# Three pairs of visits to small tensor-engine tiles joined in an attention and expert kernel

## The chip, the cores and the metric

The kernel runs on one core of one Trainium2 chip. The metric is the device time of one execution in microseconds (us); of several runs the median counts. The profiled execution is one further run of the same program.

## The reference, cut to what matters

`x` is (8, 8, 512, 64) and `state` is (8, 8, 32, 64): batch, head, position, width. Both sides read each other by attention, the two results are laid end to end along the positions, and a feed-forward layer with the mish-like gate follows.

```python
scores = scale * np.matmul(x, state.transpose(0, 1, 3, 2))
xread = softmax(scores) @ state              # (8, 8, 512, 64)
scores2 = scale * np.matmul(state, x.transpose(0, 1, 3, 2))
sread = softmax(scores2) @ x                 # (8, 8, 32, 64), "the state read"
attn = np.concatenate([xread, sread], axis=2)
x = attn.transpose(0, 2, 1, 3).reshape(8 * 544, 512)
h = x @ w_in                                 # (4352, 2048)
g = h * np.tanh(softplus(h))
out = g @ w_out                              # (4352, 512)
```

## The kernel before, in words

The work goes batch by batch (0 to 7), and each batch goes through eight **slots** of 256 columns of the hidden layer. `w_in` is folded with the state beforehand: `sw_slice` (from line 575) multiplies a slot of `w_in` with the batch's state blocks `bds[b]`, so that the first product of a slot (`gemm1`, the tile `ph`) multiplies the batch's softmax weights `ah`, `al` with that small matrix. Values are kept as a rounded part and a rest (`gh`/`gl`, `ah`/`al`, `swh`/`swl`), so most products come three times. The second product (`gemm2` in batch 0, `consume` later; tiles `acc...`) adds g times `w_out` into four PSUM banks.

Beside these full 128x128 matmuls stand **visits** to small tiles of the tensor engine, all plain f32, each of which the profile counts in two passes per matmul:

- `sw_slice`, the visit of one or two slots: weights of 64 rows and 32 columns, 16 passes for one slot and 32 for two. Its first step issues the matmuls into two banks of the pool `misc` (two banks in all), its second step copies them out on ScalarE (`act.copy` to `swh`), its third subtracts on VectorE (`dve.tensor_sub` to `swl`, or `sw` where both parts share a tile). The banks are free again after the third step.
- `scores` (from line 335), the scores of batches 1 to 7: the same 64x32 tiles, 32 passes into two banks, then a scaling of one bank on ScalarE and of the other on VectorE. It needs `xTs`, whose rows (`x_rows`) eight DMAs of `x_moved` (line 306) bring from `x_turned`, which VectorE wrote by transposing.
- `sread(kc)`, the state read: weights of 128 rows and 32 columns, 32 passes for each of two `kc`, into a bank of the pool of `ph` (two banks, `first_bank`). It needs `e2T`, which `e2_turned` (line 403) brings with 16 DMAs from `u`, which VectorE wrote by transposing the exponentials. Its second step scales on VectorE into `srds`.

**What sets the order.** Every compute engine but SyncE is wrapped in `InOrder` (line 59): each instruction is chained behind the one the program issued before on that engine. The order is written out by hand as lists of step names. Batch 0 is one long list (`hi3`, `sw6`, `SC`, ...; lower case steps are those of batch 0, `SC`, `TR`, `EX` and so on those of batch 1). Batches 1 to 7 have eight lines each in `TABLE`, one line per slot; a line that a batch lacks is taken from "steady". Naming a step once more runs its generator on to the next `yield`, so the first `S2` issues the matmuls, the second the ScalarE copies, the third the VectorE subtractions. Only the order of the DMA queue of SyncE (SP) is left to the planner of the framework; it took them here in the order of the program as they became ready.

Step names used below: `z0 z1` the state read of batch 0 (within batch 1's table), `sr0 sr1` that of the batch at hand, `SR0 SR1` that of the next batch, which the table of batch 6 uses once for batch 7, the last of its state reads. `S2` the visit of slots 2 and 3, `N0` that of slot 0 of the next batch. `mm`, `ee`, `tu`: maximum, exponential and turning (`e2_turned`) for the state read. `X0` to `X3` the four transposes to `x_turned`, `XD` the eight DMAs to `x_rows`. `A` and `B`: half of a slot's second products (in slots 0 and 1 of batch 1 they end batch 0, and each copies two results `o` out, the even one on VectorE and the odd one on ScalarE). `G0 G1` first products, `M0 M1` the activations behind them. `P p` preparing of a unit for the second product. `PR` the weights `ah`, `al`. `w0` to `w5` writes and loads of `w_in` by SP.

Of the kernel before, what the change touches and what calls it, by code (L numbers as in the profile page):

```python
# [17 lines left out]
P = 128  # L18
B, H, S, NS, D = 8, 8, 512, 32, 64
# [36 lines left out]
def half(par):  # L56
    return slice(par * D, (par + 1) * D)
# [23 lines left out]
def state_attention_mish_kernel(ctx, tc, x, state, w_in, w_out, out):  # L81
# [193 lines left out]
    def attention(b, sn, x_in=None):  # L275
# [60 lines left out]

        def scores():

            pss = [(misc if b < 3 else first_bank)(f"sc_{b}_{u}") for u in range(2)]
            for kc in range(2):  # L340
                kp = slice(kc * 2 * P, (kc + 1) * 2 * P)
                for c in range(NC):
                    o = slice(c * NS, (c + 1) * NS)
                    for u in range(2):
                        last["PE"] = pe.matmul(
                            pss[u][o, kp].rearrange("n (t v g) -> n t v g", t=NT, v=2), bds[b][half(u), kc, o],
                            xTs[c][half(u), :, kc].rearrange("p v (t g) -> p t v g", t=NT), start=True, stop=True)
            yield

            scs = pool.tile([P, 2, S], F32, tag="sc", name=f"scs_{b}", bufs=1)  # L350
            for kc in range(2):
                sc[kc] = scs[:, kc]

            for u in range(2):
                o = scs.rearrange("n k (t v u p) -> n (k t) v u p", t=NT, v=2, u=2)[:, :, :, u]
                i = pss[u].rearrange("n (k v p) -> n k v p", v=2, p=32)
                if u:
                    dve.tensor_scalar_mul(o, i, 0.125)
                else:
                    act.mul(o, i, 0.125)  # L360
                if b == 1:
                    yield
# [134 lines left out]
        def sread(kc):  # L497
# [17 lines left out]

        own = dict(
            x=x_transposed, st=lambda _: state_blocks(b, sn() if b == 1 else sn) if b else state_blocks_0(sn), sc=lambda _: scores() if b else scores_q(), tr=soft1_t, ex=soft1_x,
            no=lambda _: soft1_n(), pr=soft1_a, mm=soft2_m, ee=soft2_e, sr=sread, xd=lambda _: x_moved(), tu=lambda _: e2_turned(), fill=fill, aT=aT)

# [354 lines left out]
    for step in """  # L874
            st st st x0 x1 ldi0 x2 x3 sc hia0 ldi1 acc sc sc sc hib0 sc dia0 tr0 tr0 tr1 tr0 ldo0 tr1 jia0 cib0
            tr1 st ex0 ex1 jib0 no fill6 sw0 cib1 cia1 no coa0 ldi2 sw0 fill2 ldo1 pr0 pr0 hia1 ldi4 pr1 ldi3
            dob0 pr0 hib1 pr1 sw0 hoa0 qa0 qb0 ldo2 ldi5 jia1 jib1 di2 hob0 hi2 fill2 pr1 sw1 sw1 qb1 qa1 ji2
            ldo3 fill2 sw1 ma0 joa0 mb0 job0 ko1 ma0 mb0 wha0 sw2 p1 lx co1 loa0 sw2 la0 ci3 m1 ldo4 whb0 ga0
            lb0 sw2 lob0 ko1 ldo5 ga0 ga0 ja1 ga0 gb0 hi3 ho2 m1 ji3 gb0 gb0 lg1 ja1 gb0 p2 ci4 co2 ldo6 ldi6
            lo1 do3 sw3 g1 jo2 sw3 hi4 ji4 jo2 sw3 lo2 n2 g1 n2 X1 ho3 lg2 ldi7 g1 X2 jo3 p3 mm1 hi5 ho4 m3 sw4  # L880
            di5 g1 X3 sw4 jo3 g2 ji5 co4 sw4 g2 m3 ho5 lo3 jo4 lg3 ST X0 g2 jo4 g2 co5 sw5 p4 sw5 n4 sw5 hi6 di6
            lo4 n4 XD0 ja5 ci7 g3 g3 ja5 g3 lg4 p5 ji6 m5 g3 g4 mm0 ee0 SC SC lo5 hi7 ee1 xi2 g4 sw6 m5 g4 SC
            lg5 ldo7 sw6 TR1 g4 ji7 sw7 ho6 ee0 sw6 p6 ho7 co6 ee1 TR0 g5 TR1 g5 TR0 EX1 tu EX0 ja6 sw7 n6 co7 g5
            n6 NO xz0 sw7 ja6 g5 NO PR0 xy0 next lg6 lo6 p7 PR0 PR1 g6 g6 n7 PR0 PR1 next g6 ja7 PR1 n7
            g6 next ja7 lg7 lo7
            """.split():
        what, i = re.fullmatch(r"([a-zA-Z]+)(\d*)", step).groups()
        if not hasattr(begun.get(step), "send"):
            begun[step] = steps[what](int(i or 0))
        if hasattr(begun[step], "send"):  # L890
            next(begun[step], None)

    A12, A22, A11, A21 = range(4)
    S1, S3, S2, S4 = range(3, 7)
# [178 lines left out]
    def half_slot(key, j, at):  # L1073
# [4 lines left out]
        elif ready and (ready[0][:2] != (key, 0) or ready[0][2] < j + (j == SLOTS - 1 and at)):  # L1078
# [1 line left out]

    TABLE = {
        1: """
            G0 M0 G1 M1 z0 z1 mm0 mm1 ee0 ee1 A z0 z1 ee0 ee1 tu X0 X1
            P G0 M0 p G1 M1 w0 S2 S2 S2 X2 X3 XD B ST w1
            P G0 M0 p G1 M1
            P G0 M0 p G1 M1 S4 S6 A S4 S4 S6 S6 T0 T0
            P G0 M0 p G1 M1 sr0 sr1 SC SC A sr0 sr1 SC MM0 MM1 w2 lx TR0 TR1 TR0 TR1
# [34 lines left out]
            P G0 M0 p G1 M1 P p TR0 TR1 A P TR0 TR1 p B  # L1122
            P G0 M0 p G1 M1 S6 sr0 sr1 P p S6 S6 sr0 sr1 ly w2 EE0 EE1 EX0 EX1 A EE0 EE1 TU P p B NO
            P G0 M0 p G1 M1 P p NO PR0 PR1 A P p B
            P G0 M0 p G1 M1 N0 PR0 PR1 P p N0 N0 A P p SR0 SR1 SR0 SR1 w3 rs B U rt W0 A W1 P p""",
        B - 1: """
            P G0 M0 p G1 M1 P p A P p w4 B
            P G0 M0 p G1 M1 S2 P p S2 S2 w5 A P p B
# [133 lines left out]
```

## Time and profile before

| | before |
|---|---|
| median of 3 runs | 626.93 us (626.0 to 627.03) |
| profiled execution, its own time | 625.96 us |
| span from first to last instruction | 624.2 us |
| PE busy | 617.3 us (99%) |
| PEld (weight loads) busy | 533.9 us (86%) |
| DVE / ACT / POOL busy | 447.5 / 368.3 / 232.2 us |
| mean granted clock of TensorE | 1.000 |

PE is TensorE's matmuls, PEld its weight loads, which lie beside them; DVE is VectorE, ACT ScalarE, POOL GpSimd, SP SyncE, which here only issues DMAs. A busy share is an average; matmuls are pipelined and overlap, so the distance from one start to the next tells what one costs. In a timeline a row is: start in us, length in us, engine, line, operation, output<-inputs, shape, count; in brackets the idle time of the engine before it and what ended it ("issue": nothing that the profile shows). Nearly all rows carry line 73, that of the helper which records each operation, so tiles tell them apart.

### The profile page before, as it was taken

The numbers are of one execution on the slowest core, as the hardware profiler recorded it, in microseconds if no ns is written. First come the engines' busy times: TensorE is split into PE (matmuls) and PEld (weight loads), VectorE is DVE, ScalarE is ACT, GpSimd is POOL, SyncE is SP. The second block draws the span as 40 slices with busy tenths as digits, with TensorE's granted clock in tenths as the row PEclk, the third lists the DMA queues.
The fourth block names the chain that finished last, engine by engine and source line by source line (L and its number), as shares of the span: only waits on it lengthen the run. The fifth ranks groups of instructions, "written<-read, shape, count | busy, mean of one in ns | idle before, by whom it ended". The sixth has DMA issues, their size and how long they took to land.

```text
span 624.2 us, 13824 instructions
## 1 busy us (share of the span) xinstructions
PE 617.3 (99%) x5388; PEld 533.9 (86%) x5388; DVE 447.5 (72%) x764; ACT 368.3 (59%) x764; POOL 232.2 (37%) x348
## 2 busy tenths in 40 slices
PE   8999999999999999999999999999999999999997
PEld 6777677788888898898988898889889899898897
DVE  5999976766678885968667774869387787535364
ACT  5999876466457355565547555655456766544442
POOL 0000000235366065326632573246522744443284
PEclk9999999999999999999999999999999999999999
DMA  9995922944452163534554265415455332320011
GB/s 330 412 339 165 357 71 78 305 146 123 117 195 70 33 172 115 160 114 128 146 169 135 68 155 168 165 54 154 119 172 164 108 109 96 102 68 25 11 35 35
DMA packets 71969, 88.79 MB, mean 142 GB/s; under 512 B 13792, under 2 KB 49120, under 8 KB 71904
## 3 DMA queue, kind: packets, MB, share of 16 engines
q1 hardware_dynamic: 71472, 87.71, 44.8%
q8 instruction: 43, 0.70, 0.5%
q10 hardware_dynamic: 432, 0.20, 0.1%
q14 instruction: 22, 0.18, 0.1%
HBM read 62.85 MB, written 13.11 MB: 122 GB/s over the span
## 4 chain that ended last, share of the span: by engine, by line
PE 87%; ACT 2%; DVE 1%; DMA 1%; issue 1%; SPq 0%; DVEq 0%
PE ph L73 25%; PE acc_top L73 15%; PE acc_one L73 11%; PE acc_two L73 11%; PE acc_end L73 9%; PE swp L73 5%; PE ph_s L73 4%; PE acc L73 3%; PE srp L73 1%; PE acc_s_one L73 1%; PE acc_s_top L73 1%; PE acc_s_two L73 1%; PE sc L73 1%; DMA out_dram<-o 1%; PE acc_s_end L73 0%
## 5 line engine op out<-in xcount | busy, mean ns | idle before, releaser
L73 POOL TENSOR_TENSOR sums<-u 128x256 f32<-128x256 f32 x96 | 78.1, 814 | 194.0 <-DVE gl L73 118.8
L73 DVE TENSOR_TENSOR gl<-u,gh 128x384 fp32r<-128x384 f32 (+1 forms) x112 | 70.7, 631 | 69.5 <-ACT gh L73 62.7
L73 ACT ACTIVATE u<-ph 128x256 f32<-128x256 f32 x224 | 73.6, 382 | 79.3 <-PE ph L73 77.8
L73 POOL TENSOR_TENSOR sums<-sums,u 128x128 f32<-128x128 f32 x192 | 112.7, 587 | 15.1
L73 DVE TENSOR_TENSOR gl<-sums,gh 128x512 fp32r<-128x512 f32 x96 | 78.1, 813 | 30.6 <-ACT gh L73 30.6
L73 ACT CAST gh<-u 128x384 fp32r<-128x384 f32 (+1 forms) x112 | 59.2, 529 | 67.0 <-PE acc_end L73 49.3
L73 PE MATMUL acc_top<-wo,gh 128*128 128x256 f32 (+1 forms) x448 | 93.5, 300 | 0.0
L73 POOL TENSOR_TENSOR w_sums<-w_sums 128x256 f32<-128x256 f32 x28 | 25.2, 902 | 151.7 <-DMA x_rows<-x_turned 110.8
L73 ACT CAST gh<-sums 128x512 fp32r<-128x512 f32 x96 | 59.6, 621 | 32.2 <-POOL sums L73 32.1
L73 PEld LDWEIGHTS acc_top<-wo,gh 128*128 128x128 f32 x448 | 71.2, 191 | 4.5 <-issue 1.6
L73 PE MATMUL ph<-ah,swh 128*128 128x512 f32 (+1 forms) x228 | 70.5, 391 | 0.0
L73 PE MATMUL ph<-al,swh 128*128 128x512 f32 (+1 forms) x228 | 69.9, 388 | 0.2 <-DVE al L73 0.2
L73 PE MATMUL ph<-ah,swl 128*128 128x512 f32 (+1 forms) x228 | 69.9, 388 | 0.0
L73 PE MATMUL acc_top<-wo,gl 128*128 128x256 f32 (+1 forms) x224 | 66.9, 298 | 0.0
L73 PEld LDWEIGHTS ph<-al,swh 128*128 128x128 f32 x228 | 42.5, 188 | 10.0 <-DVE al L73 0.4
L73 PEld LDWEIGHTS ph<-ah,swl 128*128 128x128 f32 x228 | 42.6, 188 | 9.3
L73 DVE TENSOR_TENSOR swl<-swp,swh 128x512 fp32r<-128x512 f32 (+1 forms) x60 | 36.3, 645 | 18.5 <-ACT swh L73 18.5
L73 PEld LDWEIGHTS ph<-ah,swh 128*128 128x128 f32 x228 | 39.5, 188 | 8.3 <-issue 0.8
L73 PEld LDWEIGHTS acc_top<-wo,gl 128*128 128x128 f32 x224 | 42.7, 191 | 1.4
L73 ACT CAST swh<-swp 128x512 fp32r<-128x512 f32 (+1 forms) x60 | 30.5, 564 | 17.2 <-PE swp L73 17.2
L73 PE MATMUL acc<-wo,gh 128*128 128x512 f32 x128 | 40.3, 396 | 0.0
L73 PE MATMUL acc_one<-wo,gh 128*128 128x256 f32 x192 | 39.8, 289 | 0.0
(233 smaller groups left out, 1394.1 us busy)
## 6 DMA issues: line engine op xcount, KB each, us to landing
w_in<-w_in_again SPq DMA_DIRECT2D x27, 1024.0 KB, 6.1
x<-in_x_dram SPq DMA_DIRECT2D x32, 256.0 KB, 4.4
wir<-in_moe_w_in_dram SPq DMA_DIRECT2D x16, 512.0 KB, 9.4
wor<-in_moe_w_out_dram SPq DMA_DIRECT2D x16, 512.0 KB, 8.6
x_rows<-x_turned SPq DMA_DIRECT2D x56, 128.0 KB, 2.4
out_dram<-sums SPq DMA_DIRECT2D x25, 256.0 KB, 4.6
x_in<-in_x_dram SPq DMA_DIRECT2D x24, 256.0 KB, 4.8
w_in_again<-w_in_sb SPq DMA_DIRECT2D x4, 1024.0 KB, 7.5
```

What stands on the lines that cost most here:

```text
L73: made = method(*args, **kwargs)
```

## The change

Only the order of steps changes, and in one place the banks that a step takes:

- Batch 0's list: the first step of `sw6` (its matmuls) goes ahead of the two `SC` of batch 1, so that the slot visit and the scores of batch 1 follow each other on TensorE without other matmuls between. As the slot visit then holds the two `misc` banks, the scores of batch 1 take the two `first_bank` banks instead. The second and third steps of `sw6` stay where they were.
- Batch 1's table: the three steps of `S2` move from the second line into the first: the matmuls right behind `z0 z1`, the ScalarE copies behind `A`, the VectorE subtractions behind the second steps of `z0 z1` and ahead of the second steps of `ee0 ee1` and of `tu`.
- Batch 6's table, last line: `SR0 SR1` move from behind the first half of the slot's second products (`A P p`) to the place ahead of `N0`; their second steps go ahead of those of `N0`, and the load `w3` goes ahead of `A`.

```diff
-            pss = [(misc if b < 3 else first_bank)(f"sc_{b}_{u}") for u in range(2)]
+            pss = [(misc if b == 2 else first_bank)(f"sc_{b}_{u}") for u in range(2)]
...
-            lo4 n4 XD0 ja5 ci7 g3 g3 ja5 g3 lg4 p5 ji6 m5 g3 g4 mm0 ee0 SC SC lo5 hi7 ee1 xi2 g4 sw6 m5 g4 SC
+            lo4 n4 XD0 ja5 ci7 g3 g3 ja5 g3 lg4 p5 ji6 m5 g3 g4 mm0 ee0 sw6 SC SC lo5 hi7 ee1 xi2 g4 m5 g4 SC
             lg5 ldo7 sw6 TR1 g4 ji7 sw7 ho6 ee0 sw6 p6 ho7 co6 ee1 TR0 g5 TR1 g5 TR0 EX1 tu EX0 ja6 sw7 n6 co7 g5
...
         1: """
-            G0 M0 G1 M1 z0 z1 mm0 mm1 ee0 ee1 A z0 z1 ee0 ee1 tu X0 X1
-            P G0 M0 p G1 M1 w0 S2 S2 S2 X2 X3 XD B ST w1
+            G0 M0 G1 M1 z0 z1 S2 mm0 mm1 ee0 ee1 A S2 z0 z1 S2 ee0 ee1 tu X0 X1
+            P G0 M0 p G1 M1 w0 X2 X3 XD B ST w1
             P G0 M0 p G1 M1
             P G0 M0 p G1 M1 S4 S6 A S4 S4 S6 S6 T0 T0
             P G0 M0 p G1 M1 sr0 sr1 SC SC A sr0 sr1 SC MM0 MM1 w2 lx TR0 TR1 TR0 TR1
...
-            P G0 M0 p G1 M1 N0 PR0 PR1 P p N0 N0 A P p SR0 SR1 SR0 SR1 w3 rs B U rt W0 A W1 P p""",
+            P G0 M0 p G1 M1 SR0 SR1 N0 PR0 PR1 P p SR0 SR1 N0 N0 w3 A P p rs B U rt W0 A W1 P p""",
```

## Rows read from the trace of the kernel before

**Rows 1.** The page: busy time of the engines, and the granted clock in 40 slices
```profile
PE 617.3 (99%) x5388; PEld 533.9 (86%) x5388; DVE 447.5 (72%) x764; ACT 368.3 (59%) x764; POOL 232.2 (37%) x348
...
PEclk9999999999999999999999999999999999999999
```

**Rows 2.** Timeline of PE in batch 0: scores of batch 1, slots 6 and 7
```profile
62.69 1.09 PE L73 MATMUL sc<-x_rows,bd 64*32 64x256 f32 x32
63.72 0.73 PE L73 MATMUL acc<-wo,gh 128*128 128x512 f32 x2
...
64.98 0.39 PE L73 MATMUL acc<-wo,gl 128*128 128x512 f32 x1
65.48 0.67 PE L73 MATMUL swp<-w_in_sb,bd 64*32 64x256 f32 x16
66.08 0.73 PE L73 MATMUL acc<-wo,gh 128*128 128x512 f32 x2
...
68.70 0.39 PE L73 MATMUL acc<-wo,gl 128*128 128x512 f32 x1
69.02 0.66 PE L73 MATMUL swp<-w_in_sb,bd 64*32 64x256 f32 x16
```

**Rows 3.** Timeline of DVE in the same stretch
```profile
63.92 0.69 DVE L73 TENSOR_SCALAR scs<-sc 128x512 f32<-128x512 f32 x1 [0.38 <-PE sc L73]
...
66.52 1.23 DVE L73 SCALAR_TENSOR_TENSOR w_in_sb<-wir 128x1024 uint32<-128x1024 uint32 x1 [0.15 <-ACT wir L73]
...
67.92 0.74 DVE L73 TENSOR_TENSOR sw<-swp,sw 128x256 fp32r<-128x256 f32 x2
...
77.31 0.75 DVE L73 TENSOR_TENSOR sw<-swp,sw 128x256 fp32r<-128x256 f32 x2
```

**Rows 4.** Timeline of ACT, the longest idle time of this stretch
```profile
71.68 2.17 ACT L73 ACTIVATE wor<-wor 128x1024 f32<-128x1024 f32 x2 [2.94 <-DMA wor<-in_moe_w_out_dram]
```

**Rows 5.** Timeline of PEld, the next visit (slots 0 and 1 of batch 1)
```profile
78.08 0.65 PEld L73 LDWEIGHTS swp<-w_in_sb,bd 64*32 64x32 f32 x32 [0.35 <-DVE sw L73]
```

**Rows 6.** Timeline of PE, batch 1 slot 4: state read, then scores of batch 2
```profile
114.17 1.19 PE L73 MATMUL srp<-x_again,e2T 128*32 128x64 f32 x64
115.29 1.14 PE L73 MATMUL sc<-x_rows,bd 64*32 64x256 f32 x32
116.36 0.73 PE L73 MATMUL acc_top<-wo,gh 128*128 128x512 f32 x2
```

**Rows 7.** Timeline of ACT, batch 1 slots 0 and 1
```profile
94.56 0.59 ACT L73 COPY o<-acc 128x512 f32<-128x512 f32 x1 [0.57 <-PE acc L73]
...
98.36 1.07 ACT L73 CAST sw<-swp 128x512 fp32r<-128x512 f32 x2 [0.16 <-PE swp L73]
```

**Rows 8.** Timeline of DVE, batch 1 slots 0 and 1
```profile
94.19 0.14 DVE L73 TENSOR_SCALAR sm<-sm 128x1 f32<-128x1 f32 x1
...
94.69 1.28 DVE L73 STREAM_TRANSPOSE u<-e 128x512 f32<-128x512 f32 x2
...
98.98 1.29 DVE L73 TENSOR_TENSOR sw<-swp,sw 128x512 fp32r<-128x512 f32 x2 [1.24 <-ACT sw L73]
```

**Rows 9.** Timeline of the DMA queue of SP, batch 1 slots 0 to 4
```profile
96.05 10.96 SPq L403 DMA_DIRECT2D e2T<-u  x16
107.12 5.19 SPq L306 DMA_DIRECT2D x_rows<-x_turned  x8
```

**Rows 10.** Tile x_rows: landing of its issues begun at 111.1 and 111.7
```profile
DMA to landing us min/median/max: 2.7/3.0/3.2
```

**Rows 11.** Chain that ended last, batch 6 slot 7: slot 0 visit, state read
```profile
484.46 1.02 PE swp L73 x32
...
488.19 1.03 PE srp L73 x64
```

**Rows 12.** Timeline of the DMA queue of SP, batch 6 slots 6 and 7
```profile
473.29 11.09 SPq L403 DMA_DIRECT2D e2T<-u  x16
```

**Rows 13.** Tile e2T: landing of its issues begun at 483.1 and 483.8
```profile
DMA to landing us min/median/max: 1.8/1.8/1.8
```

## The prediction, made before the changed kernel was run

> **What bounds the kernel now.** I read the page first: TensorE is busy for 99% of the span and its granted clock stands in the top tenth in every slice [rows 1], which is its level of 2.4 GHz. So a microsecond in which TensorE waits is lost at the end, and one that it saves is kept only if it meets no later wait. The question is thus not what the visits cost but whether, after the move, each still finds its inputs and banks ready. That is read from timelines of the three stretches, engine by engine, and from the DMA queue.
>
> **What joining can save.** In batch 0 the scores (32 passes) start at 62.69 and the next ordinary matmul at 63.72, so 1.03 us; the slot visit (16 passes) takes 65.48 to 66.08, 0.60 us [rows 2]. Sixteen passes more cost 0.43, so 48 in one go take 1.46, and 0.17 is saved. Ordinary starts there lie 0.227 apart: behind one visit six matmuls separate 63.72 from 64.98 (5 starts, 1.26), behind the other twelve separate 66.08 from 68.70 (11 starts, 2.62), so six starts take 1.36. The first matmul behind a visit costs 1.26 - 5 x 0.227 = 0.13 extra, the entry into one 69.02 - 68.70 - 0.227 = 0.09 extra. One visit less in one tile shape saves 0.17 + 0.13 + 0.09 = 0.39 us. The slot visit also began 65.48 - 64.98 = 0.50 after the matmul ahead of it, where 0.32 is usual: it waited 0.18 for the scores' banks, and that wait goes too. On TensorE alone the first join gains 0.57.
>
> The other two joins put a state read (128x32 tiles) ahead of a slot visit (64x32). State read and scores joined take 114.17 to 116.36, 2.19 [rows 6]. Apart, visit and read take 1.02 and 1.03 [rows 11]. So the join costs 0.14 more in passes and saves one exit and entry, 0.22: 0.08 net.
>
> The Trainium skill, "TensorEngine Tiling (Array Packing)", section Tiling Modes, says that a change of tiling mode drains TensorE. The trace agrees for the step from tiles to ordinary matmuls (0.13 and 0.09 extra); between read and scores, also two modes, 1.12 us against 1.03 leave about 0.09 for it. By the rule with a full exit and entry there (0.22), these two joins would save nothing, which alters the sum by 0.1.
>
> **First join: batch 0's scores with slot 6.** Slot 6's subtractions end at 67.92 + 0.74 = 68.66, and slot 7's visit, which needs the same two banks, started at 69.02 [rows 2, 3]. It would now come at 68.45. But VectorE's scaling at 63.92 had waited for the scores [rows 3]; with slot 6's passes ahead of them the scores end 0.43 later. VectorE has 0.15 of idle time ahead of 66.52, so the subtractions end about 0.28 later, at 68.94, and slot 7 starts at 69.0, as before. Even if it did not, the next visit at 78.08 needs slot 7's banks, which VectorE frees at 77.31 + 0.75 = 78.06, behind work on ScalarE that waited 2.94 us for a load of w_out [rows 3, 4, 5]; TensorE's order doesn't move that load. I take 0.0; bounds -0.57 (all kept) and +0.3 (VectorE's delay carried on).
>
> **Second join: S2 moved ahead by a slot.** What is gained on TensorE is 0.08. What is moved past is more. VectorE's subtractions of S2 now stand ahead of `ee`'s second steps and of `tu`, whose transposes feed 16 DMAs. Step by step, with the joined visit lasting as the scores do (116.36 - 115.29 = 1.07, so 1.08 with rounding):
> - ScalarE's copy of `o` at 94.56 waits for TensorE [rows 7] and comes at 95.64.
> - S2's two copies follow some 0.48 behind it, at 96.12. Before, the subtractions began 98.98 - 98.36 = 0.62 after the copies [rows 7, 8], so now at 96.74, and hold VectorE for 1.2 of their 1.29 us, to 97.94.
> - Only then come `sm` and its like, which stood at 94.19, and 0.50 later the transposes to `u`, which stood at 94.69 [rows 8]: 98.44 instead, 3.75 later.
> - SP began the 16 issues of e2T at 96.05 as soon as `u` was there; they take 10.96 us, and the eight of x_rows follow directly, at 107.12, for 5.19 [rows 9]. Both shift by 3.75: the queue is full from one end to the other and gives nothing back.
> - The last x_rows issue, at 111.7, took up to 3.2 to land [rows 10], 114.9; the scores of batch 2 started at 115.29 [rows 6], so 0.4 was spare. Now the landing is at 118.65, and the scores, otherwise due at 115.2, start at 118.7. That is +3.4 us. With the group's 2.7 for the landing it is +2.9.
> The state read ahead of it stays free: its last DMA was issued at 107.0 at the latest, is now at 110.8 and lands within 2 us if it does as those of [rows 13], before 114.17. Queued behind the waiting scores on TensorE is everything; SP's next DMAs (stores, writes and loads of w_in) come 3.75 later too, beside work that is 3.4 later itself. Below, the bound is -0.1 (no wait at all); above, +3.8, the whole shift.
>
> **Third join: batch 7's state read ahead of N0.** The 16 DMAs of its e2T are issued from 473.29 to 484.38; the last starts at 483.8 and lands 1.8 later, at 485.6 [rows 12, 13]. The read was at 488.19 and had 2.6 to spare; it now stands where N0 stood, at 484.46 [rows 11]. It waits about 1.25 us. The move itself saves 0.08. The load w3, which needs the read's x buffer, goes out some 2 us earlier; I cost that at nothing, since what uses it comes in the last stage, behind a load issued before it. Its cover gone, it would cost no more than now. The second steps wait behind the read on VectorE, which has idle time there. I take +1.2; bounds -0.1 and +1.4.
>
> **Sum.** 0.0 + 3.4 + 1.2 = +4.6 us, less 0.1 for small waits around the last stage that find more room: +4.5. Against the profiled execution's 625.96 that gives 630.5; the median of the runs shown is 0.97 above it, so 626.93 + 4.5 = **631.4**.
>
> **Rivals.**
> 1. *Only part of the second wait.* If the scores' input lands with less delay (the planner sending `tu` ahead of the subtractions), only TensorE's 1.08 of delay ahead of `o` moves e2T; the wait falls to 115.99 + 0.05 - 115.29, about +0.7. Total 0.7 + 1.2 = +1.9, 628.8. Against it: VectorE's rows stand in the order of the program, which chains each engine. Chance 0.10.
> 2. *No wait, not slower.* The place is SP's issue pace, now 0.69 per e2T issue and 0.65 per x_rows issue [rows 9]. Both waits go if the 24 issues behind 99.8 fit ahead of the reads: (115.2 - 2.7 - 99.8) / 23, 0.55 or less per issue [rows 10], and (484.4 - 1.8 - 473.29) / 15 = 0.62 for the third join. Then the joins' 0.16 is left: 626.8, within 0.2%. For it: nothing else is in SP's way. Against it: the two e2T groups of the rows agree within 2% (10.96 and 11.09) [rows 9, 12]. It also covers a change that does nothing measurable. Chance 0.12.
> 3. *The clock falls.* TensorE would stand idle for some 3.5 us ahead of the scores, which it does nowhere now, and its granted clock stood at the top throughout [rows 1]. If it fell to 1.2 GHz for as long as TensorE had stood, the work of 1.75 us would take twice that: +1.75, 633.1. The Trainium skill, "TensorE: Matmul & The Clock Gate", section HAM oscillation, says that idle gaps in the matmul stream bring the clock to half; no run here shows it. Chance 0.08.
> 4. *All of the first join kept and no wait*: 626.93 - 0.57 - 0.16, 626.2; with a little more elsewhere it is faster by over 0.2%. Against it stand the two bank waits of [rows 3, 5]. Chance 0.04.
>
> **How the numbers follow.** A measurement here can tell about 0.2%, 1.25 us, from no change. The forecast has 0.66; it, rivals 1 and 3 are slower: 0.84. Rival 2 is within: 0.12. Rival 4 is faster: 0.04. The range takes in rival 1 and reaches just past rival 3; rivals 2 and 4, 0.16, stay outside: 628.2 to 633.2.
>
> **What would show it.** In the changed trace: e2T's issues in batch 1 start near 99.8, not 96.05; PE idles about 3.5 us between state read and scores near 115, released by the DMA of x_rows, and about 1.2 us ahead of the last state read, released by e2T; slot 7's visit in batch 0 still starts near 69.0. I am wrong if the scores follow the read without a gap, or if e2T still starts near 96.

## The result, and the profile after

The changed kernel takes **632.98 us** (median of 4 runs, 632.7 to 633.42) against 626.85 (626.0 to 627.03) for the kernel before in runs beside it: ratio 1.0096, 95% interval 1.0084 to 1.0108, 6.1 us slower. Forecast was 631.4, with 628.2 to 633.2 around it. Its profiled execution took 633.42, span 631.6; that of before had 624.2. The page, against [rows 1]:

```profile
PE 619.3 (98%) x5388; PEld 535.5 (85%) x5388; DVE 446.9 (71%) x764; ACT 368.3 (58%) x764; POOL 233.2 (37%) x348
...
PEclk9999999899999999999999999999999999999999
```

The same 5388 matmuls keep PE busy 2.0 us longer in a span 7.4 longer. So 5.4 us are idle time and 2.0 are slower or longer matmuls, and one slice of the clock, the eighth, is no longer at the top. The list of PE's waits says where the idle time lies (us in total, times, longest):

```profile
PE sc L73 <- DMA x_rows<-x_turned: 3.0, 1, 3.0
PE srp L73 <- DMA e2T<-u: 1.4, 1, 1.4
...
PE acc_one L73 <- DVE wx_w_in L73: 1.2, 1, 1.2
```

The first two are new; the third stood at 0.4 in the list of before. They belong to joins 2 and 3, and to a place that the change does not touch.

**Join 1: nothing gained.** PE in batch 0, answering to [rows 2]:

```profile
62.86 0.66 PE L73 MATMUL swp<-w_in_sb,bd 64*32 64x256 f32 x16
63.31 1.11 PE L73 MATMUL sc<-x_rows,bd 64*32 64x256 f32 x32
...
68.81 0.99 PE L73 MATMUL swp<-w_in_sb,bd 64*32 64x256 f32 x16
69.73 0.74 PE L73 MATMUL ph<-ah,sw 128*128 128x512 f32 x2
```

The last of these lines in the kernel before:

```profile
69.61 0.74 PE L73 MATMUL ph<-ah,sw 128*128 128x512 f32 x2
```

DVE there, answering to [rows 3]:

```profile
64.53 0.69 DVE L73 TENSOR_SCALAR scs<-sc 128x512 f32<-128x512 f32 x1 [0.78 <-PE sc L73]
...
68.26 0.74 DVE L73 TENSOR_TENSOR sw<-swp,sw 128x256 fp32r<-128x256 f32 x2
```

The joint visit is there. The scaling waits 0.78 for the scores instead of 0.38, and the subtractions come at 68.26 instead of 67.92; half of these 0.34 us is the start of the stretch, which stands 0.17 later in this execution (62.86, before 62.69). The next visit, slot 7's, starts its first passes early, at 68.81, but lasts 0.99 instead of 0.66: it has one bank and waits behind its first matmul for the other, which the second subtraction frees at 69.00. From the start of the small visit to the first product behind slot 7 it is 6.87 us; before it was 6.92 (62.69 to 69.61).

**Join 2: 5.3 us lost.** From the subtractions of S2 to the eight x_rows transfers, on DVE and then on the queue of SP, answering to [rows 8, 9]:

```profile
96.71 1.29 DVE L73 TENSOR_TENSOR sw<-swp,sw 128x512 fp32r<-128x512 f32 x2 [1.39 <-ACT sw L73]
...
98.42 1.28 DVE L73 STREAM_TRANSPOSE u<-e 128x512 f32<-128x512 f32 x2
```

```profile
99.78 10.91 SPq L403 DMA_DIRECT2D e2T<-u  x16
110.79 6.33 SPq L306 DMA_DIRECT2D x_rows<-x_turned  x8
```

The first issue of e2T moved from 96.05 to 99.78, the first of x_rows from 107.12 to 110.79. The eight x_rows last 1.1 longer as a group, but only by the issue of the last one, 1.65 us instead of 0.60, behind which no other of them stands. The last three of them, and how long they took to land:

```profile
L306 SPq DMA_DIRECT2D x_rows<-x_turned x3: 599/615/1652, 114.2 to 115.5; - x3
DMA to landing us min/median/max: 3.5/3.7/3.9
```

PE, answering to [rows 6]:

```profile
113.97 1.28 PE L73 MATMUL srp<-x_again,e2T 128*32 128x64 f32 x64
118.21 0.59 PE L73 MATMUL sc<-x_rows,bd 64*32 64x256 f32 x2 [2.97 <-DMA x_rows<-x_turned]
119.08 1.50 PE L73 MATMUL sc<-x_rows,bd 64*32 64x256 f32 x30 [0.28 <-issue]
120.51 1.22 PE L73 MATMUL acc_top<-wo,gh 128*128 128x512 f32 x2
...
124.54 0.62 PE L73 MATMUL ph<-ah,swh 128*128 128x512 f32 x2
```

And PE in the kernel before, where [rows 6] don't show it:

```profile
90.39 1.19 PE L73 MATMUL srp<-x_again,e2T 128*32 128x64 f32 x64
...
119.22 0.61 PE L73 MATMUL ph<-ah,swh 128*128 128x512 f32 x2
```

Between state read and scores PE stands idle for 2.97, then 0.28 more, which ends as the last x_rows lands (115.5 + 3.5 = 119.0). The `ph` at 124.54 stood at 119.22 before: 5.32 later, while the start of the earlier read `z0 z1` is the same to 0.01 (90.40, 90.39). The length of the ordinary pairs tells that not all of it is waiting: 1.22 against 0.73 in [rows 6]. Windows (us; then busy time of PE, PEld, DVE, ACT, POOL with counts; granted clock; DMA share; GB/s):

```profile
118.20:119.00 0.80, 0.59 (x2) 0.12 (x2) 0.00 (x0) 0.00 (x0) 0.00 (x0) 1.00 1.02 335
119.00:120.00 1.00, 0.92 (x30) 0.58 (x30) 0.00 (x0) 0.00 (x0) 0.00 (x0) 0.81 0.92 346
120.00:121.00 1.00, 1.00 (x15) 0.49 (x2) 0.35 (x1) 0.39 (x1) 0.00 (x0) 0.50 1.07 414
...
123.00:124.00 1.00, 1.00 (x6) 0.82 (x5) 1.00 (x2) 0.00 (x0) 0.00 (x0) 0.98 1.05 403
```

The granted clock falls to half (1.2 GHz) behind the idle time, when work has begun again, and is back at 2.4 GHz at about 123.

**Join 3: 1.3 us lost.** PE in batch 6's last slot, answering to [rows 11]:

```profile
490.50 0.31 PE L73 MATMUL srp<-x,e2T 128*32 128x64 f32 x6
492.23 1.05 PE L73 MATMUL srp<-x,e2T 128*32 128x64 f32 x58 [1.42 <-DMA e2T<-u]
...
502.10 1.09 PE L73 MATMUL ph_s<-srT,wh 128*128 128x512 f32 x4
```

The two ends of this stretch in the kernel before:

```profile
484.39 1.09 PE L73 MATMUL swp<-w_in,bd 64*32 64x256 f32 x32
...
494.66 1.09 PE L73 MATMUL ph_s<-srT,wh 128*128 128x512 f32 x4
```

From the first small visit to `ph_s` it is 11.60; before it was 10.27 (484.39 to 494.66): 1.33 more. Six passes find their e2T in place, the other 58 wait for the last of the 16 transfers. The granted clock does not fall behind this idle time (1.00 from 490 to 500).

**The sum.** 0 + 5.3 + 1.3 = 6.6, and 0.8 at the wait for `wx_w_in`, 7.4 between the two spans. The last term is no effect of the change: the runs below that change nothing there show 1.04 to 1.38 in that place. The profiled execution of before had a short wait there and was the fastest of its runs. The medians, 6.1 apart, say nearly the same as the joins.

### The profile page after: what moved, and what is told of

The parts are those of the page before. It is cut to its first block, busy times and chain, and to the rows that moved or that the text cites. A ratio compares the mean times of both kernels' runs of the same rounds, so it can differ in the third digit from the quotient of the medians.

```text
span 631.6 us, 13829 instructions
## 1 busy us (share of the span) xinstructions
PE 619.3 (98%) x5388; PEld 535.5 (85%) x5388; DVE 446.9 (71%) x764; ACT 368.3 (58%) x764; POOL 233.2 (37%) x348
## 4 chain that ended last, share of the span: by engine, by line
PE 90%; DMA 4%; SPq 3%; DVE 2%; issue 1%; ACT 1%; DVEq 0%
PE ph L73 25%; PE acc_top L73 14%; PE acc_one L73 11%; PE acc_two L73 10%; PE acc_end L73 8%; PE acc L73 7%; PE swp L73 5%; PE ph_s L73 4%; SPq L403 2%; PE sc L73 1%; DMA w_in<-w_in_again 1%; PE srp L73 1%; PE acc_s_one L73 1%; PE acc_s_top L73 1%; PE acc_s_two L73 1%; DMA out_dram<-o 1%
## 5 line engine op out<-in xcount | busy, mean ns | idle before, releaser
L73 POOL TENSOR_TENSOR sums<-sums,u 128x128 f32<-128x128 f32 x192 | 114.2, 595 | 15.1
```

Of the source, the lines that this page charges most:

```text
L73: made = method(*args, **kwargs)
```

## The experiments

Each was timed beside runs of the kernel before on the same chip, whose medians were 627.57 (beside the first four), 627.53 (the next four), 627.89 and 627.45 us.

### One join at a time

Join 1 alone:

```diff
-            pss = [(misc if b < 3 else first_bank)(f"sc_{b}_{u}") for u in range(2)]
+            pss = [(misc if b == 2 else first_bank)(f"sc_{b}_{u}") for u in range(2)]
...
-            lo4 n4 XD0 ja5 ci7 g3 g3 ja5 g3 lg4 p5 ji6 m5 g3 g4 mm0 ee0 SC SC lo5 hi7 ee1 xi2 g4 sw6 m5 g4 SC
+            lo4 n4 XD0 ja5 ci7 g3 g3 ja5 g3 lg4 p5 ji6 m5 g3 g4 mm0 ee0 sw6 SC SC lo5 hi7 ee1 xi2 g4 m5 g4 SC
```

> Only the first join (slot 6 of batch 0 ahead of batch 1's scores). Theory: its gain on TensorE, 0.57 us, is swallowed at once, since slot 7's visit waits for the banks that VectorE frees later: slot 7 starts within 0.2 us of 69.0, the next visit within 0.2 of 78.1, and the time is that of before within 0.3 us (0.05%). Rival: the gain is kept, slot 7 starts at 68.5, and the time falls by 0.4 to 0.6 us.

Measured: 627.67, ratio 1.0005 [0.9991, 1.0019]. PE in batch 0:

```profile
63.60 0.66 PE L73 MATMUL swp<-w_in_sb,bd 64*32 64x256 f32 x16
...
70.48 0.74 PE L73 MATMUL ph<-ah,sw 128*128 128x512 f32 x2
```

6.88 us from the joint visit to `ph`, against 6.92 before. The absolute times are some 0.7 later than expected; PE had waited 0.8 for `xT` at the start of batch 0 in this execution, 50 us earlier; within the stretch slot 7's visit (69.56) starts 5.96 behind the joint visit, as in the changed kernel (5.95). The join keeps nothing: the second bank gives the start of slot 7's visit, as forecast.

Join 2 alone (the two lines of batch 1's table, as in the change):

> Only the second join (S2 a slot earlier). Theory: all of the large loss is here: e2T's issues start near 99.8, TensorE idles some 3 us ahead of the scores of batch 2 and its granted clock falls to half for some 3.5 us behind that; time +4.5 to +6.0 us against before. Rival: the loss comes from the three joins together (batch 0's later VectorE work included); then this one alone costs clearly less, +3 or below.

Measured: 632.99 (630.87 to 634.23), ratio 1.0078 [1.005, 1.0106]. PE, then windows:

```profile
118.53 2.67 PE L73 MATMUL sc<-x_rows,bd 64*32 64x256 f32 x32 [3.22 <-DMA x_rows<-x_turned]
...
125.38 0.62 PE L73 MATMUL ph<-ah,swh 128*128 128x512 f32 x2
```

```profile
115.30:118.50 3.20, 0.00 (x1) 0.01 (x1) 0.00 (x0) 0.00 (x0) 1.63 (x3) 0.81 0.71 191
118.50:119.50 1.00, 0.97 (x10) 0.46 (x18) 0.00 (x0) 0.00 (x0) 0.00 (x0) 0.50 1.05 390
...
121.00:124.00 3.00, 3.00 (x14) 2.30 (x8) 2.69 (x6) 0.60 (x1) 0.00 (x0) 0.50 1.05 395
```

This join makes 4.9 of the 6.1 us. The scores start at 118.53, beside the forecast's 118.7, though no issue of x_rows took longer than 0.65 us in this execution; landings of up to 4.1 us (3.2 before) came without a long issue. Here the clock fell within the idle time: 0.81 on average from 115.3 to 118.5, and 0.50 from the scores' first pass on. From the scores to `ph` it takes 6.85 us, where before it took 3.93 (115.29 to 119.22): 2.92 more, with the clock at half for most of it. Four of the five runs had a mean clock of 0.995 to 0.997 and took 631.74 to 634.23; the fifth kept 1.000 and took 630.87, 3.3 above before, which is what the waiting alone was forecast to cost. That is one run, and its trace was not kept.

Join 3 alone (the line of batch 6's table, as in the change):

> Only the third join (batch 7's state read ahead of N0). Theory: the read waits for the last e2T pieces, 1.2 to 1.5 us, the granted clock stays at the top level; time +1.1 to +1.5 us against before. Rival: the wait only takes the place of slack in the last stage, and the time is within 0.4 us of before.

Measured: 628.43, ratio 1.0018 [1.0001, 1.0035], so 1.1 us. PE in batch 6's last slot:

```profile
485.49 0.31 PE L73 MATMUL srp<-x,e2T 128*32 128x64 f32 x6
487.04 1.05 PE L73 MATMUL srp<-x,e2T 128*32 128x64 f32 x58 [1.23 <-DMA e2T<-u]
```

In place it is 11.42 (485.49 to 496.91) against 10.27, 1.15 more. Singly, the joins give 0.3 + 4.9 + 1.1 = 6.3 by their ratios, together 6.1: no sign that they act on each other, as far as their intervals, 0.9 to 1.8 us to either side, can tell.

### The clock, taken out of join 2

The changed kernel with 14 matmuls on the identity, whose results nobody reads, behind the state read:

```diff
-            P G0 M0 p G1 M1 sr0 sr1 SC SC A sr0 sr1 SC MM0 MM1 w2 lx TR0 TR1 TR0 TR1
+            P G0 M0 p G1 M1 sr0 sr1 FL SC SC A sr0 sr1 SC MM0 MM1 w2 lx TR0 TR1 TR0 TR1
...
+        def filler():
+            pt = first_bank("fl")
+            for _ in range(14):
+                pe.matmul(pt[:, :P], ident, ident, start=True, stop=True)
...
```

> All three joins, and 14 f32 matmuls of 128 columns on a spare bank between the state read and the scores of batch 2, where TensorE waited; their output is not used. Theory: the scores start when their rows land, near 119 as without the filling, but the granted clock stays at 2.4 GHz, and what follows is about 1.3 to 1.7 us earlier: +4.5 to +4.9 us against before in place of +6.1. Rival: the slow matmuls behind the wait are due to something else (contention with the loads at 120 to 123), and the time stays within 0.4 us of +6.1.

Measured: 633.28 (632.99 to 634.34), ratio 1.0093 [1.0068, 1.0119]; by the whole time no gain shows, so the expectation was missed there. PE, then a window:

```profile
114.94 1.28 PE L73 MATMUL srp<-x_again,e2T 128*32 128x64 f32 x64
116.14 3.39 PE L73 MATMUL fl<-ident 128*128 128x128 f32 x28
...
120.28 1.09 PE L73 MATMUL sc<-x_rows,bd 64*32 64x256 f32 x30 [0.20 <-issue]
121.30 0.73 PE L73 MATMUL acc_top<-wo,gh 128*128 128x512 f32 x2
...
124.16 0.62 PE L73 MATMUL ph<-ah,swh 128*128 128x512 f32 x2
```

```profile
120.00:122.00 2.00, 1.80 (x34) 1.18 (x34) 0.52 (x1) 0.57 (x1) 0.00 (x0) 1.00 0.99 379
```

The clock stays at 1.00, though the DMA engines are about as busy as in the changed kernel (0.99 against 1.07): it is not their traffic that made the matmuls slow there. From the 30 passes to `ph` it takes 3.88 instead of 5.46 in the changed kernel, 1.58 less; the passes themselves come 0.23 later behind the read, as the transfers landed later, so 1.35 remain from `srp` to `ph`. In this execution the state read came 0.97 later than in the changed kernel's profile (114.94 against 113.97), and PE's waits for the first loads of batch 0 account for most of it: 0.76 against 0.16. That is how the two spans come to be equal, 631.6. Three of the four runs kept a mean clock of 1.00 and still took 632.99 to 633.38, and for the two of them that were not profiled nothing says where the gain went. The place shows the clock's price; the whole time, by four runs, does not.

### Other places for the same joins

The join of S2 kept, but its second and third steps put at the end of the line, behind `tu`:

```diff
-            G0 M0 G1 M1 z0 z1 mm0 mm1 ee0 ee1 A z0 z1 ee0 ee1 tu X0 X1
-            P G0 M0 p G1 M1 w0 S2 S2 S2 X2 X3 XD B ST w1
+            G0 M0 G1 M1 z0 z1 S2 mm0 mm1 ee0 ee1 A z0 z1 ee0 ee1 tu X0 X1 S2 S2
+            P G0 M0 p G1 M1 w0 X2 X3 XD B ST w1
```

> Only the second join, and the copies and subtractions of S2 stand behind tu and the first two transposes, not ahead of them; the visits on TensorE are joined as in the change. Theory (the subtractions ahead of tu held the DMAs back): e2T's issues start 1.1 us later than in the kernel before, near 97.1, not 3.75; the scores of batch 2 wait about 0.9 us or less, the granted clock stays at the top level; time +0.5 to +1.3 us against before, where the join as made cost about +5. Rival (joining the visits is itself what is dear, whatever VectorE does): +3 us or more.

Or the turning put ahead of `A` and the subtractions last:

```diff
-            G0 M0 G1 M1 z0 z1 mm0 mm1 ee0 ee1 A z0 z1 ee0 ee1 tu X0 X1
-            P G0 M0 p G1 M1 w0 S2 S2 S2 X2 X3 XD B ST w1
+            G0 M0 G1 M1 z0 z1 S2 mm0 mm1 ee0 ee1 ee0 ee1 tu A S2 z0 z1 X0 X1 S2
+            P G0 M0 p G1 M1 w0 X2 X3 XD B ST w1
```

> Only the second join, and the second steps of ee and tu go ahead of A's copies too, so that VectorE's transposes to u wait for nothing of TensorE; S2's subtractions come behind the first transposes of x. Theory: e2T's issues start within 0.4 us of 96.0, the scores of batch 2 follow the state read without a gap, and the join's small gain is left: 0 to -0.3 us against before. Rival: something else of the join holds the x rows (the DMA queue, the transposes of x that come later), and TensorE still waits 0.5 us or more ahead of the scores.

Measured: medians of 629.31 and 628.79 against 627.53, runs of 627.27 to 630.4 and 626.93 to 630.04, for both a ratio of 1.0014 [0.9998, 1.0031]. The second was expected at or below before and by the medians missed that; the first was expected to keep the top clock and did not. In each the large wait is gone. PE in the second of them:

```profile
114.09 1.19 PE L73 MATMUL srp<-x_again,e2T 128*32 128x64 f32 x64
115.21 1.15 PE L73 MATMUL sc<-x_rows,bd 64*32 64x256 f32 x32
...
159.16 0.39 PE L73 MATMUL acc_one<-wx_w_in,gh 128*128 128x256 f32 x1 [2.26 <-DVE wx_w_in L73]
```

e2T starts at 97.41 and 95.73 (99.78 in the changed kernel), and the scores follow the read directly (in the first their passes then take 0.29 longer than before). So the 5 us hang on where VectorE's two subtractions and `tu` stand, not on the joint visit. From `z0 z1` to the state read the second takes 23.62 (90.47 to 114.09), before it took 23.78: the join's own gain is 0.16. The traces agree on it: the seven with this join show 23.56 to 23.63, the five without it 23.78 to 23.84. It does not arrive. The wait for `wx_w_in` near 158 grew to 1.82 and 2.26, and the clock fell behind it in both (second kernel):

```profile
162.00:163.50 1.50, 1.50 (x5) 1.21 (x5) 1.50 (x4) 0.61 (x1) 0.00 (x0) 0.50 0.68 160
```

ScalarE shows where a part of the second one's wait comes from:

```profile
123.64 0.84 ACT L73 CAST wx_w_in<-w_sums 128x768 fp32r<-128x768 f32 x1 [0.62 <-DMA w_in_again<-w_in_sb]
```

Before, this cast came at 122.98 with no wait. It holds up the exponentials behind it, and with them the next 16 issues of e2T (136.25; before 135.59), the loads and the stores of `o` behind those, the VectorE step that waits for the stores, and the writing of `wx_w_in`. That is 0.66 of the 1.90 by which the wait grew over that of before. Another 0.72 is the 16 issues themselves, 10.95 us against 10.23; they took 10.92 to 11.12 in the three kernels that leave the table of batch 1 alone (e1, e3, e7), where the wait was 1.04 to 1.38.

Join 3 with the slot visit first and the read second:

```diff
-            P G0 M0 p G1 M1 N0 PR0 PR1 P p N0 N0 A P p SR0 SR1 SR0 SR1 w3 rs B U rt W0 A W1 P p""",
+            P G0 M0 p G1 M1 N0 SR0 SR1 PR0 PR1 P p N0 N0 SR0 SR1 w3 A P p rs B U rt W0 A W1 P p""",
```

> Only the third join, with the slot visit N0 ahead of the state read and not behind it. Theory: the 1.0 us of the visit covers most of the wait for e2T: the read waits 0.2 to 0.5 us in place of 1.2 to 1.4, and with one exit and entry saved the time is within 0.4 us of before, about 1.1 below the join as made. Rival: the wait for e2T has other causes that move with the read, and it stays above 0.8 us.

Measured: 627.78, ratio 1.0 [0.9987, 1.0013]. PE:

```profile
486.25 1.09 PE L73 MATMUL swp<-w_in,bd 64*32 64x256 f32 x32
487.27 1.49 PE L73 MATMUL srp<-x,e2T 128*32 128x64 f32 x64
...
496.55 1.09 PE L73 MATMUL ph_s<-srT,wh 128*128 128x512 f32 x4
```

10.30 in place, as before (10.27). The visit covers most of the landing; what is left makes the read 0.4 longer (1.49 against 1.10) and takes the gain of the join.

### The wait near 158 by itself

To see whether the small wait that took e6's gain can be removed: e6's table, with batch 2's `T2` steps (which write `wx_w_in`) moved ahead of the transposes:

```diff
-            P T2 G0 M0 p G1 M1 P p X0 X1 A T2 T2 P X2 X3 p B
+            P T2 G0 M0 p G1 M1 P p T2 T2 X0 X1 A P X2 X3 p B
```

> The second join as in the run before (ee and tu ahead), and in batch 2's first slot the low parts of the summed weights of T2 are taken ahead of the first two transposes of x on VectorE. TensorE waits for them near 157 in every trace so far, 0.36 to 1.38 us. Theory: that wait goes, the scores of batch 2 don't wait, and the time is 0.5 to 1.5 us below before. Rival: the wait is set by the landing of the stored results, which come first on VectorE, so that it stays or moves to the next use of the summed weights, and the time is within 0.4 us of before.

Measured: 626.78 (625.65 to 627.91), ratio 0.998 [0.9967, 0.9993]; the wait is 0.90, so it did not go as expected, but the clock stays up. Then, on top of that, the stores of `o` ahead of the four x loads (step `li`) in SP's queue:

```diff
-            P G0 M0 p G1 M1 PR0 PR1 P p PR0 A N0 N2 N0 N0 PR1 li P p B""",
+            P G0 M0 p G1 M1 PR0 PR1 P p PR0 A N0 N2 N0 N0 PR1 P p B li""",
...
-                load_x_in(global_next)
+                with ExitStack() as st:
+                    if key == 1:
+                        st.enter_context(behind("store"))
+                    load_x_in(global_next)
```

> The run before (second join with ee and tu ahead, T2's low parts ahead), and at the end of batch 1 the two stores of results go out on the DMA queue of SP ahead of the four loads of x for batch 3, not behind them. Theory: VectorE's wait for the landing of the stores (4.4 to 5.6 us in every trace so far) shortens by 2 us or more, TensorE no longer waits near 157, none of the runs has the fall of the granted clock there; time 1.0 to 2.0 us below before. Rival: the loads of x, now later, hold the transposes of x and with them VectorE, and TensorE waits as long there; time within 0.5 us of the run before.

Measured: **625.81** (625.36 to 626.36), ratio 0.996 [0.9945, 0.9975], the lowest median of all kernels here. SP, then VectorE:

```profile
146.88 1.90 SPq L693 DMA_DIRECT2D out_dram<-o  x2
148.83 1.99 SPq L136 DMA_DIRECT2D x_in<-in_x_dram  x4
```

```profile
151.43 0.56 DVE L73 TENSOR_TENSOR gl<-u,gh 128x384 fp32r<-128x384 f32 x1 [1.43 <-DMA out_dram<-o]
```

In the changed kernel that VectorE step waited 5.23 for the same stores, in that of before 4.43, and in e8, which differs from this one only in this order, 5.16; now 1.43, and `acc_one` follows without a wait. Last, both of these edits without any join:

> The kernel before with the last run's two other edits alone (T2's low parts ahead, the stores ahead of the loads), no visits joined. Theory: the gain of the last run came from the wait near 157 and not from the join, so this one stands within 0.5 us of it, 1.5 to 2.2 us below before, without the fall of the granted clock in any run. Rival: the join had its part; then this one is slower than the last run by over 0.5 us.

Measured: 626.0 (625.13 to 627.48), ratio 0.998 [0.9969, 0.9991], and no wait for `wx_w_in` in the trace. So the two edits gain without the join. How the two share the gain was not tried. Nor can it be told whether the join adds its 0.16: the medians of the two last kernels are 0.2 apart, on different chips, their ratios 0.2%, and the intervals overlap. One run of the twelve had a mean clock of 0.997 (627.48, the slowest), which was not expected.

## Why the prediction was right, and where it was not

**First join, 0.0: right, for the reason given.** Slot 7's visit waits for a bank that VectorE frees (68.26 + 0.74 = 69.00, forecast 68.94; in place, with the 0.17 of the later start taken off, 68.83), and e1 keeps nothing. A detail was not seen: a visit may start with one free bank and wait inside, so its start (68.81) shows less than its length.

**Second join, +3.4: the chain was right, the size was not; it is 5.3.** Subtractions at 96.71 (forecast 96.74), `u` at 98.42 (98.44), e2T at 99.78 (99.80), the state read without a wait: each step was met to 0.03. Two things were mis-sized. The last x_rows took longer to land than the forecast's 3.2: the last two were issued at 114.8 and 115.5, the latter about as forecast (115.4), and landed 3.7 and 3.5 behind that. The bulk of the scores began at 119.08 instead of 118.7; as two passes were done by then this makes 0.3. The other 1.58 is the clock.

The step that failed is the choice between forecast and rival 3: the forecast took the top clock for what follows an idle stretch, since [rows 1] show nothing else. Those rows show no idle stretch of that length either, so they could not speak for it. Rival 3 priced the fall at 1.75 by doubling the work of half the idle time; its total of 633.1 is what was measured, at a chance of 0.08. That its size fits is partly luck: it took the half clock to last as long as the idle time, some 3.5 us, and by the windows it lasted about 3.4 us of work in the changed kernel (from some 119.6 to 123.0) but about 5.6 in e2 (118.5 to some 124.1), an estimate from the mean clocks. The measured time stands in the forecast's range only 0.2 below its upper end, and because the range was drawn to take in rival 3; the forecast itself is 1.6 too low, and a quarter of the loss, the clock's 1.58 us, came by a step that it had put at nothing.

The Trainium skill, "TensorE: Matmul & The Clock Gate", section HAM oscillation, has idle gaps in the matmul stream bring the clock to half; here the trace agrees, 0.50 behind 2.97 us.

**Third join, +1.2: right, with a slip in its sum.** From the landing at 485.6 to the place at 484.46 it is 1.14, not the 1.25 that was set down. The wait is 1.42, as the 16 issues took 11.46 instead of 11.09; the loss is 1.33 in the changed kernel and 1.15 alone. The 0.1 taken off for the last stage isn't seen: from `ph_s` to the end it is 129.5 in both kernels. As to the cause, e7 shows that the order within the joint visit makes it.

**Rivals.** Rival 1 fell (tu kept its place behind the subtractions, and e5 shows what it would have taken to free it). Rival 2 fell: SP needed 0.68 per issue of e2T (10.91 / 16), not 0.55. Rival 4 fell with e1.

**The joins' own saving** was put at 0.08, or at nothing if a change between two tile shapes cost a full exit and entry. Measured: 0.16 in e6, 0.21 in the changed kernel (23.57 from `z0 z1` to `sr0 sr1`, before 23.78). A change between these two tile shapes thus costs less here than going out to ordinary matmuls and back; it alters little in the sum. The Trainium skill, "TensorEngine Tiling (Array Packing)", section Tiling Modes, has a change of tiling mode drain TensorE; the trace agrees for the way out to ordinary matmuls and back, 0.22 us in the prediction's rows.

**What stays open.** Why the last x_rows took up to 3.9 us to land in the changed kernel and 4.1 in e2, the 0.3 above; the issue of 1.65 us is not it, as one of 1.49 stands in e10, where no landing took longer than 3.3. And how idle time and the fall of the clock go together: in the profiles the clock fell with waits of 1.82, 2.26, 2.97 and 3.22 us and not with those of 0.36 to 1.61 (the last in e4, at the third join), which is a list and not a rule. Of 91 repeat runs of the kernel before, 15 had a mean clock of 0.997 and took 629.1 to 630.4 us, the others 626.0 to 629.5; e5's and e6's profiled runs, where the clock fell near 160, had 0.997 too. That the kernel before loses its clock there now and then, and that e9 is faster because it does not (1.00 or 0.999 in all its 10 runs), is argued from this and not shown: none of those runs of before was profiled, and e10, without that wait in its trace, has one run of 0.997.

## What to carry to other kernels

Joining small visits saved some 0.2 us, while every step hung behind the moved one shifts by microseconds: follow the vector steps, the queue of transfers that they start, and the banks, and do it before counting passes. A queue that is full from end to end hands a late start on (here 3.73 us at e2T, 3.67 at x_rows), so what starts it must not stand behind work that nobody waits for. Price an idle stretch of TensorE higher than its length where the granted clock may fall, as it did with those of 1.82 to 3.22 us here; and where a tuned kernel waits for a store, look at the order of the transfer queue first.

## What was not expected of the hardware

- The half clock need not come in the idle time. In the changed kernel it came after it: 1.00 in the window in which work began again, 0.81 in the next, then 0.50 until about 123, over 3 us of work. In e2 it came before work began again, and the scores ran at 0.50 from their first pass. So nearly the same idle time cost 1.58 in one execution and 2.92 in the other.
- The 16 issues of e2T took between 10.01 (batch 1 of e6) and 12.36 us (batch 6 of e10) with the same shapes.
- The same stores cost the step that waits for them 1.43 us of idle time where they stand ahead of four loads in the queue (e9) and 5.16 where they stand behind (e8).
